# A dense first product from quarters by seven products, the conversion's words in PSUM, and a slot's result copied by ScalarE

## The chip, the cores and the metric

The kernel runs on one core of a Trainium2 chip, as one launch. The metric is the device time of that launch in microseconds. TensorE (PE) multiplies, VectorE (DVE) and ScalarE (ACT) work elementwise on the two on-chip memories SBUF and PSUM, GpSimd (POOL) works on SBUF and issues DMAs, SyncE (SP) issues DMAs. PE's results land in PSUM, which has eight banks.

## What is computed

Three stages follow each other: attention reads of 8 x 8 heads, a routed mixture of 8 experts over 4608 rows, and a dense two-layer network over the same rows:

```python
x = np.ascontiguousarray(attn_out.transpose(0, 2, 1, 3)).reshape(B * S, H * D)   # 4608 x 512
...
for e in range(E):                       # 8 experts, w1 512 x 1024, w2 1024 x 512
    mask = expert_idx == e
    h = np.maximum(x[mask] @ w1[e], 0.0)
    out[mask] = gate_w[mask, None] * (h @ w2[e])
...
h = x @ w_in                             # 4608 x 512 by 512 x 2048
r = np.maximum(h, 0.0)
g = s * (r * r) + b
return (g @ w_out).astype(np.float32)    # 2048 x 512
```

## The kernel before

Products are made of 32-bit values split in two parts, `hi` (what PE's fp32r format holds) and `lo` (the rest): each product is three matmuls, hi-hi, hi-lo and lo-hi, each with a weight load of its own, all accumulated in PSUM. The order on every engine is that in which the code is written.

**Attention and routing** (`phase_a`, to about 140 us) writes the rows sorted by expert to `Xs` in device memory.

**Experts** (`phase_b`, about 140 to 630 us). The rows lie in 38 slots of 128. One turn of the loop over slots (L998) issues: the first product of slot s (`mm1`, 24 matmuls of 512 columns), the columns of slot s+1 (`xcols`: DVE transposes 32 x 32 blocks, L919, ACT copies `hi`, L924, DVE makes `lo`, L925), the second product of slot s-1 (`mm2`, 24 matmuls into `yp`, two buffers), DVE's copy of that result out of PSUM (L975), and the transposes of slot s's hidden values with their parts (`hcols`: PE L949, ACT L954, DVE L955). Beside it POOL loads the experts' weights into a ring of two experts in SBUF, `R[m, part, unit]`, and makes their `lo` parts by `TENSOR_TENSOR` (L702), four operations in a row.

The dense weights come as 64-bit floats and are converted to 32 bits in the same loop, one piece of 512 columns in each of slots 2 to 33 (16 pieces of `w_in`, then 16 of `w_out`): a DMA loads the words into `dbl`, `conv_bits` (L715) makes from the high and low words a value `c_a` and a remainder `c_m` with five DVE operations on SBUF tiles, `conv_split` (L735) makes `hi` (ACT) and `lo` (DVE), and SP's DMAs write both to `Wc` in device memory. When an expert's half of the ring is free, `dense_load` (L749) brings `Wc` into it: `w_in` at the end of the expert stage, `w_out` at the start of the dense one. `dense_done` counts up a semaphore for each quarter, on which PE waits (`wait_prep`).

**Dense** (`phase_c`, from about 630 us). Block 0 has two tiles of 128 rows (256 columns), blocks 1 to 8 four (512 columns). For each of 16 `f` (128 hidden columns) `mm1` (L1104) makes the first product in one of two PSUM buffers: 4 pieces of the inner dimension x 3 matmuls. ACT and DVE make relu, square and the parts `gh`, `gl`; `mm2` (L1125) adds 12 matmuls to `po`, four PSUM buffers, 3 `f` later (`skew`, 5 in block 0). During a block the next block's rows are gathered (POOL), gated (DVE), moved in 32 x 32 blocks (16 DMAs) and transposed (DVE); `ycols` makes their parts. Block 1's columns are transposed by PE instead.

Of the kernel before, what the change touches and what calls it, by code (L numbers as in the profile page):

```python
# [51 lines left out]
class Kern:  # L52
# [4 lines left out]
    def consts(self):  # L57
# [5 lines left out]
        self.Wc = dp.tile([2, 2, P, 8192], F32, name="Wc")  # L63
# [28 lines left out]
        self.flag2 = T([P, 1], "flag2")  # L92
        self.endI = T([1, NE + 1], "endI", I32)
# [621 lines left out]
    def conv_bits(self, c, wp):  # L715

        nc = self.nc
        raw = self.cv[c]
        T = lambda name: wp.tile([P, 512], I32, name="c_" + name, bufs=1)
# [5 lines left out]
        v.tensor_scalar(out=q.bitcast(F32), in0=H.bitcast(F32), scalar1=2.0 ** -112, scalar2=None, op0=ALU.mult)  # L725
        v.tensor_scalar(out=s, in0=H, scalar1=-0x80000000, scalar2=None, op0=ALU.bitwise_and)

        v.scalar_tensor_tensor(out=a, in0=q, scalar=3, in1=s, op0=ALU.logical_shift_left, op1=ALU.bitwise_or)

        v.tensor_scalar(out=s, in0=a, scalar1=-0x800000, scalar2=None, op0=ALU.bitwise_and)  # L730
        b, A = q.bitcast(F32), a.bitcast(F32)
        v.scalar_tensor_tensor(out=b, in0=L, scalar=2.0 ** -36, in1=s.bitcast(F32), op0=ALU.mult, op1=ALU.mult)
        self.cv[c] = A, b

    def conv_split(self, c, wp):  # L735

        nc = self.nc
        v = nc.vector
        m, o = c // 16, (c % 16) * 512
        A, b = self.cv.pop(c)  # L740
        hi = wp.tile([P, 512], F32R, name="c_hi", bufs=1)
        lo = wp.tile([P, 512], F32R, name="c_lo", bufs=1)
        nc.scalar.copy(hi, A)
        v.tensor_tensor(out=A, in0=A, in1=hi.bitcast(F32), op=ALU.subtract)
        v.tensor_tensor(out=lo, in0=A, in1=b, op=ALU.add)
        nc.sync.dma_start(self.Wc[m, 0, :, o:o + 512], hi.bitcast(F32))
        nc.sync.dma_start(self.Wc[m, 1, :, o:o + 512], lo.bitcast(F32))

    def dense_load(self, m, h, wait=False):  # L749

        nc, tc = self.nc, self.tc
        u = h // 2
        if wait:
            c = self.endI[0:1, NE - 2:NE - 1] if m == 0 else self.endI[0:1, NE:NE + 1]
            v = nc.gpsimd.value_load(c, min_val=1, max_val=NSLOT)  # L755
            self.pool_wait(self.d2 if u else self.d1, v)
        x = slice((h % 2) * 2048, (h % 2) * 2048 + 2048)
        for hl in range(2):
            k = nc.gpsimd.dma_start(self.R[:, m, hl, u, x], self.Wc[m, hl, :, h * 2048:(h + 1) * 2048])
# [73 lines left out]
    def places(self, wp):  # L833
# [3 lines left out]
        T = lambda name: wp.tile(B, F32, name="p_" + name)  # L837
# [3 lines left out]
        y, t = V("y"), T("t")  # L841
# [4 lines left out]
        def rows():  # L846
            d = V("d")
# [9 lines left out]
            for nm, w in (("a", wa), ("b", wb), ("c", wc)):  # L857
                v = V(nm)
                nc.vector.tensor_tensor(out=t, in0=self.oh, in1=bc(w), op=ALU.mult)
# [8 lines left out]
        def gates():  # L868
            u, r = V("u"), V("r")
# [15 lines left out]
    def phase_b(self):  # L885
# [6 lines left out]
        with ExitStack() as cx:  # L892
            yps = cx.enter_context(tc.tile_pool(name="yps", bufs=2, space=PSUM))
# [18 lines left out]
            def xcols(s, plain=False):  # L912
# [4 lines left out]
                else:  # L917
                    p = w.tile([P, DM], F32, name="xT", bufs=1)
# [26 lines left out]
            def hcols(s):  # L945
# [4 lines left out]
                hi = w.tile([P, 8, P], F32R, name="hhi")  # L950
                lo = w.tile([P, 8, P], F32R, name="hlo")
# [7 lines left out]
            def mm2(s, ks=range(8)):  # L959
# [15 lines left out]
                nc.vector.tensor_copy(y, p)  # L975
# [16 lines left out]
            places = self.places(wb1)  # L992
# [5 lines left out]
            for s in range(1, NFULL + 1):  # L998
# [24 lines left out]
                if s == C0 + NC:  # L1023
                    z = w.tile([P, DM], I32, name="c_m", bufs=1).bitcast(F32)
# [3 lines left out]
                    for h in range(4):  # L1028
                        self.dense_load(0, h, h % 2 == 0)
                    self.dense_done(0, range(4))  # L1030
# [16 lines left out]
    def phase_c(self):  # L1047
        nc, tc, i = self.nc, self.tc, self.i
        R = self.R
        with ExitStack() as cx:  # L1050
            ops = cx.enter_context(tc.tile_pool(name="ops", bufs=1, space=PSUM))
            h2p = cx.enter_context(tc.tile_pool(name="h2p", bufs=2, space=PSUM))
            t2p = cx.enter_context(tc.tile_pool(name="t2p", bufs=2, space=PSUM))
            w = cx.enter_context(tc.tile_pool(name="wC", bufs=2))
            NF = F2 // P
            blocks = [list(ST)] + [[xt(b, j) for j in range(4)] for b in range(NB)]
            G = {}
# [31 lines left out]
            def ycols(bl, k, first=False):  # L1089
                n = len(bl)  # L1090
                if first:
                    p = t2p.tile([P, 4, P], F32, name="yt")[:, :n, :]
                    for j in range(n):
                        nc.tensor.transpose(p[:, j, :], G["g"][:, j, k * P:(k + 1) * P], self.ident)  # L1094
                else:
                    p = G["yT"][:, :n, :].rearrange("p n (i k t) -> p k n i t", i=4, k=4)[:, k]
                hi = w.tile([P, 4, P], F32R, name="yhi", bufs=4)
                lo = w.tile([P, 4, P], F32R, name="ylo", bufs=4)
                v = lambda a: a[:, :n, :] if first else a[:, :n, :].rearrange("p n (i t) -> p n i t", i=4)
# [4 lines left out]
            def mm1(yt, f, n):  # L1104
                p = h2p.tile([P, 4, P], F32, name="h2")
                for k in range(4):
                    o = (f // 8) * 4096 + k * 1024 + (f % 8) * P
                    win = R[:, 0, :, :, :].rearrange("p a b c -> p (a b c)")
                    hi, lo = win[:, o:o + P], win[:, 8192 + o:8192 + o + P]
                    yh, yl = yt[k][0][:, :n, :], yt[k][1][:, :n, :]  # L1110
                    self.mm(p[:, :n, :], hi, yh, k == 0, False)
                    self.mm(p[:, :n, :], hi, yl, False, False)
                    self.mm(p[:, :n, :], lo, yh, False, k == 3)
                r = w.tile([P, 4, P], F32, name="r2", bufs=3)
                r_ = r[:, :n, :]
                nc.scalar.activation(r_, p[:, :n, :], AF.Relu)  # L1116
                nc.vector.scalar_tensor_tensor(out=r_, in0=r_, scalar=self.s_sb, in1=r_, op0=ALU.mult, op1=ALU.mult)  # L1117
                gh = w.tile([P, 4, P], F32R, name="gh", bufs=6)
                gl = w.tile([P, 4, P], F32R, name="gl", bufs=6)
                nc.scalar.activation(gh[:, :n, :], r_, AF.Identity, bias=self.b_sb, scale=1.0)  # L1120
                nc.vector.scalar_tensor_tensor(out=gl[:, :n, :], in0=r_, scalar=self.b_sb,  # L1121
                                               in1=gh[:, :n, :].bitcast(F32), op0=ALU.add, op1=ALU.subtract)
                return gh, gl

            def mm2(po, g, f, js):  # L1125
                wo = R[:, 1, :, :, :].rearrange("p a b c -> p (a b c)")
                o = f * 512
                hi, lo = wo[:, o:o + 512], wo[:, 8192 + o:8192 + o + 512]
                for j in js:
                    self.mm(po[j], g[0][:, j, :], hi, f == 0, False)  # L1130
                    self.mm(po[j], g[0][:, j, :], lo, False, False)
                    self.mm(po[j], g[1][:, j, :], hi, False, f == NF - 1)
# [12 lines left out]
            for t in range(len(blocks[0])):  # L1145
                gather(blocks[0], t)
            for h in range(4):
                self.dense_load(1, h, h % 2 == 0)
            self.dense_done(1, range(4))
            gated(blocks[0], True)  # L1150
            self.warm(t2p, "yt", 25)
            yt = [ycols(blocks[0], k, True) for k in range(4)]
            for bi, bl in enumerate(blocks):
                n = len(bl)
                nxt = blocks[bi + 1] if bi + 1 < len(blocks) else []
                skew = 5 if bi == 0 else 3
                po = [ops.tile([P, DM], F32, name=f"po{j}") for j in range(n)]
                q = []
                for f in range(NF):
                    if bi == 0 and f % 8 == 0:  # L1160
                        self.wait_prep(2 * (f // 8) + 1)
                    q.append(mm1(yt, f, n))
                    if f >= skew:
                        ff = f - skew
                        if bi == 0 and ff % 4 == 0:
                            self.wait_prep(4 + ff // 4)
                        mm2(po, q[ff], ff, range(n))
                    if 4 <= f < 4 + len(nxt):
                        gather(nxt, f - 4)
                    if f == (9 if bi else 13):  # L1170
# [77 lines left out]
```

## Time and profile before

| | |
|---|---|
| median of 3 runs | 1411.25 us (1409.95 to 1422.62) |
| profiled execution | 1412.1 us, span 1410.3 us from first to last instruction |
| PE busy | 1364.0 us, 97% of the span |
| DVE / ACT / POOL busy | 715.3 / 419.2 / 333.3 us |
| mean granted PE clock | 0.990 |
| moved by DMA | 197.18 MB, mean 140 GB/s |

The matmuls are pipelined: the duration of one in a row is longer than the distance from one to the next, so prices per matmul are taken from the start of the first to the start of the last of many. A DVE operation's row gives its duration; two that do not wait for each other overlap by some hundredths of a microsecond.

### The profile page before, as it was taken

How to read it: one execution, taken by the hardware profiler on the slowest of the kernel's cores; microseconds unless marked ns; L12 is line 12 of the kernel's file. 1: busy time of each engine (PE TensorE's matmuls, PEld its weight loads, DVE VectorE, ACT ScalarE, POOL GpSimd, SP SyncE). 2: the span in 40 equal slices, each digit the busy share in tenths (PEclk: the TensorE clock that was granted, in tenths of full speed). 3: DMA queues.
4: the chain of work that ended last, by engine and by line, in shares of the span. 5: the costliest groups of instructions: out<-in, count | busy, mean ns of one | idle time of the engine just before them, and what ended most of it. 6: DMA issues, size and time to landing. Idle time of an engine off the chain costs nothing.

```text
span 1410.3 us, 19618 instructions
## 1 busy us (share of the span) xinstructions
PE 1364.0 (97%) x6469; PEld 1084.9 (77%) x6469; DVE 715.3 (51%) x1194; ACT 419.2 (30%) x748; POOL 333.3 (24%) x380
## 2 busy tenths in 40 slices
PE   8898999988999989999999999999999999999998
PEld 5666777777778768868888888888888888888887
DVE  6687566888775787423433334233342343433322
ACT  4666222222222222213322223222232232322321
POOL 3777633656430653103001000010000100100000
PEclk9999999999999999999999999999999999999999
DMA  9895886988873895727102021020110201101000
GB/s 331 294 353 188 261 278 222 326 298 296 294 241 123 292 310 172 276 76 287 35 3 58 30 45 46 0 61 30 30 60 0 60 31 28 62 1 31 31 0 30
DMA packets 94289, 197.18 MB, mean 140 GB/s; under 512 B 14952, under 2 KB 49768, under 8 KB 84464
## 3 DMA queue, kind: packets, MB, share of 16 engines
q1 hardware_dynamic: 77776, 98.34, 22.0%
q0 software_dynamic: 16384, 97.53, 19.8%
q8 instruction: 61, 1.00, 0.3%
q14 instruction: 36, 0.29, 0.1%
q10 hardware_dynamic: 32, 0.02, 0.0%
HBM read 140.53 MB, written 47.97 MB: 134 GB/s over the span
## 4 chain that ended last, share of the span: by engine, by line
PE 54%; DMA 0%; issue 0%; DVE 0%; ACT 0%; POOL 0%; POOLq 0%; ACTq 0%
PE h L784 27%; PE po L784 27%; DMA y<-Ys,pos 0%; PE yt L1094 0%; ACT yhi L1100 0%; DVE ob L1136 0%; POOL y L1062 0%; DVE yz L1071 0%; DVE ylo L1101 0%; POOLq L755 0%; POOLq L1062 0%; ACTq L1100 0%
## 5 line engine op out<-in xcount | busy, mean ns | idle before, releaser
L784 PE MATMUL h<-yhi,ring 128*128 128x512 f32 (+1 forms) x1152 | 365.1, 384 | 0.5 <-ACT yhi L1100 0.5
L784 PE MATMUL po<-ring,gh 128*128 128x512 f32 x1088 | 342.7, 396 | 0.0
L1117 DVE SCALAR_TENSOR_TENSOR r<-r,s_sb 128x512 f32<-128x512 f32 (+1 forms) x144 | 103.9, 721 | 330.5 <-ACT r L1116 330.5
L784 PEld LDWEIGHTS h<-yhi,ring 128*128 128x128 f32 x1152 | 214.0, 189 | 47.7 <-ACT yhi L1100 0.7
L784 PEld LDWEIGHTS po<-ring,gh 128*128 128x128 f32 x1088 | 203.7, 188 | 48.2 <-issue 0.2
L784 PE MATMUL h<-ylo,ring 128*128 128x512 f32 (+1 forms) x576 | 221.1, 384 | 0.0
L784 PE MATMUL po<-ring,gl 128*128 128x512 f32 x544 | 215.3, 396 | 0.0
L784 PE MATMUL hp<-ring,xhi 128*128 x592 | 193.3, 408 | 16.2 <-ACT xhi L924 15.3
L1116 ACT ACTIVATE r<-h 128x512 f32<-128x512 f32 (+1 forms) x144 | 83.0, 576 | 377.6 <-PE h L784 377.5
L784 PE MATMUL yp<-ring,hhi 128*128 x592 | 186.7, 396 | 0.0
L702 POOL TENSOR_TENSOR ring<-raw,ring 128x512 fp32r<-128x512 f32 x112 | 149.0, 1362 | 90.8 <-DMA ring<-in_moe_w_dram 90.5
L1062 POOL DMA_INDIRECT y<-Ys,pos x34 | 35.1, 1033 | 542.0 <-DMA yz<-y 333.7
L1121 DVE SCALAR_TENSOR_TENSOR gl<-r,b_sb,gh 128x512 fp32r<-128x512 f32 (+1 forms) x144 | 103.9, 722 | 110.7 <-ACT gh L1120 110.7
L784 PEld LDWEIGHTS hp<-ring,xhi 128*128 128x128 f32 x592 | 111.0, 192 | 42.3 <-ACT xhi L924 17.0
L1120 ACT ACTIVATE gh<-r,b_sb 128x512 fp32r<-128x512 f32 (+1 forms) x144 | 100.9, 701 | 114.0 <-DVE r L1117 114.0
L784 PEld LDWEIGHTS yp<-ring,hhi 128*128 128x128 f32 x592 | 111.5, 189 | 26.9
L784 PEld LDWEIGHTS h<-ylo,ring 128*128 128x128 f32 x576 | 109.0, 189 | 24.3
L784 PEld LDWEIGHTS po<-ring,gl 128*128 128x128 f32 x544 | 102.4, 188 | 25.0
L784 PE MATMUL yp<-ring,hlo 128*128 x296 | 117.9, 398 | 3.7 <-DVE hlo L955 3.7
L784 PE MATMUL hp<-ring,xlo 128*128 x296 | 119.5, 404 | 0.0
L954 ACT CAST hhi<-ht 128x512 fp32r<-128x512 f32 x74 | 43.5, 587 | 161.7 <-PE ht L949 89.1
L955 DVE TENSOR_TENSOR hlo<-ht,hhi 128x512 fp32r<-128x512 f32 x74 | 51.0, 690 | 44.3 <-ACT hhi L954 44.3
(226 smaller groups left out, 1289.9 us busy)
## 6 DMA issues: line engine op xcount, KB each, us to landing
ring<-in_moe_w_dram POOLq DMA_DIRECT2D x32, 1024.0 KB, 9.4
raw<-in_moe_w_dram POOLq DMA_DIRECT2D x28, 1024.0 KB, 5.6
ring<-Wc POOLq DMA_DIRECT2D x16, 1024.0 KB, 12.3
Ys<-y SPq DMA_DIRECT2D x38, 256.0 KB, 2.1
xs<-Xs SPq DMA_DIRECT2D x148, 64.0 KB, 4.4
xT<-in_x_dram SPq DMA_DIRECT2D x16, 512.0 KB, 6.1
xr<-in_x_dram SPq DMA_DIRECT2D x16, 512.0 KB, 7.6
dbl<-in_moe_w_in_dram SPq DMA_DIRECT2D x16, 512.0 KB, 5.5
```

The source lines that it names most:

```text
L702: self.own(nc.gpsimd.tensor_tensor(out=lo[:, x], in0=raw[:, c:c + 512], in1=hi[:, x].bitcast(F32), op=ALU.subtract))
L784: k = nc.tensor.matmul(out, lhsT=l, rhs=r, start=start, stop=stop)
L954: nc.scalar.copy(hi[:, x, :], p[:, x, :])
L955: nc.vector.tensor_tensor(out=lo[:, x, :], in0=p[:, x, :], in1=hi[:, x, :].bitcast(F32), op=ALU.subtract)
L1062: nc.gpsimd.indirect_dma_start(out=G["y"][:, j, :], out_offset=None, in_=self.Ys, in_offset=bass.IndirectOffsetOnAxis(ap=self.pos[:, bl[j] ...
L1116: nc.scalar.activation(r_, p[:, :n, :], AF.Relu)
L1117: nc.vector.scalar_tensor_tensor(out=r_, in0=r_, scalar=self.s_sb, in1=r_, op0=ALU.mult, op1=ALU.mult)
L1120: nc.scalar.activation(gh[:, :n, :], r_, AF.Identity, bias=self.b_sb, scale=1.0)
L1121: nc.vector.scalar_tensor_tensor(out=gl[:, :n, :], in0=r_, scalar=self.b_sb, in1=gh[:, :n, :].bitcast(F32), op0=ALU.add, op1=ALU.subtract)
```

## The change

Lines beginning with "-" are those of before. The diff is cut to what matters for the time.

```diff
 conv_bits:
-        q, a, s = T("m"), T("a"), T("s")
+        a = wp.tile([P, 512], I32, name="c_a", bufs=1)
+        q = self.cps.tile([P, 512], I32, name="cx")
 ...
+        v.tensor_scalar(out=b, in0=H.bitcast(F32), scalar1=2.0 ** -112, scalar2=None, op0=ALU.mult)
+        v.tensor_scalar(out=q, in0=q, scalar1=3, scalar2=None, op0=ALU.logical_shift_left)
+        v.scalar_tensor_tensor(out=a, in0=H, scalar=-0x80000000, in1=q, op0=ALU.bitwise_and, op1=ALU.bitwise_or)
+        v.tensor_scalar(out=q, in0=a, scalar1=-0x800000, scalar2=None, op0=ALU.bitwise_and)
+        v.scalar_tensor_tensor(out=b, in0=L, scalar=2.0 ** -36, in1=b, op0=ALU.mult, op1=ALU.mult)
 conv_split:
+        if 2 <= c < 18:
+            self.conv_parts(self.V[:, 2 * h:2 * h + 2, :], self.Wi[:, i - 1, 4 + 2 * h:6 + 2 * h, :], wp)
+        x = self.cps.tile([P, 2, 256], F32, name="cy")
+        v.tensor_tensor(out=x.rearrange("p a b -> p (a b)"), in0=A, in1=b, op=ALU.add)
 ...
+        self.conv_parts(x, self.Wi[:, i, 2 * h:2 * h + 2, :], wp)
+        if h == 0:
+            nc.scalar.copy(W, x)
+            v.tensor_tensor(out=V[:, 0, :], in0=x[:, 1, :], in1=W[:, 0, :], op=ALU.subtract)
+        else:
+            v.tensor_tensor(out=V[:, 3, :], in0=x[:, 1, :], in1=W[:, 0, :], op=ALU.add)
+            v.tensor_tensor(out=V[:, 1, :], in0=V[:, 3, :], in1=W[:, 1, :], op=ALU.subtract)
+            v.tensor_tensor(out=V[:, 2, :], in0=x[:, 0, :], in1=V[:, 1, :], op=ALU.subtract)
+    def conv_parts(self, x, dst, wp):
+        t = wp.tile([P, 2, 512], F32R, name="c_hl")
 ...
+        nc.scalar.copy(hi, x)
+        nc.vector.tensor_tensor(out=lo, in0=x, in1=hi.bitcast(F32), op=ALU.subtract)
+        nc.sync.dma_start(dst, t.bitcast(F32))
 phase_b:
-            yps = cx.enter_context(tc.tile_pool(name="yps", bufs=2, space=PSUM))
+            yps = cx.enter_context(tc.tile_pool(name="yps", bufs=1, space=PSUM))
+            cps = self.cps = cx.enter_context(tc.tile_pool(name="cps", bufs=1, space=PSUM))
 ...
-                    p = w.tile([P, DM], F32, name="xT", bufs=1)
+                    p = xps.tile([P, 4, P], F32, name="tp").rearrange("p a b -> p (a b)")
 ...
-                nc.vector.tensor_copy(y, p)
+                nc.scalar.copy(y, p)
+                nc.vector.tensor_copy(self.flag3, y[:, DM - 1:])
 phase_c:
+            def sums():
 ...
+                for o, a, b in ((t1, b12, b11), (t2, b22, t1), (t3, b22, b12), (t4, b21, t2)):
+                    nc.gpsimd.tensor_tensor(out=o, in0=a, in1=b, op=ALU.subtract)
+                return b11, t2, t3, t1, b21, t4, b22
+            def mm1(yt, n):
 ...
+                a, b, c, d = [hq.tile([P, 2, HT], F32, name=x) for x in "abcd"]
 ...
+                prod(a[:, 0], A11, B11)
+                nc.scalar.copy(s1[:, 0], a[:, 0])
+                prod(b[:, 0], S2, T2)
+                add(u2[:, 0], s1[:, 0], b[:, 0])
+                prod(c[:, 0], S3, T3)
+                prod(c[:, 1], S1, T1)
+                add(u34, u2.to_broadcast([P, 2, HT]), c)
+                add(y[:, 1], u34[:, 0], c[:, 1])
+                prod(d[:, 0], A22, T4)
+                prod(d[:, 1], S4, B22)
+                add(x, u34, d)
+                prod(a[:, 1], A12, B21)
+                add(y[:, 0], s1[:, 0], a[:, 1])
+            def wload(n):
 ...
+                    nc.sync.dma_start(Rw[:, o:o + WB].bitcast(F32),
+                                      self.Wi[:, n % NP, 1:8, :].rearrange("p q x -> p (q x)"))
 ...
+                skew = 1 if bi else 3
 ...
+                for i in range(NP):
 ...
+                        m = (bi - 1) * NP + i
+                        q.append(mm1(yt, m))
+                        wload(m + NBUF)
+                    if i >= skew:
+                        second(i - skew, range(n))
 ...
+                        if i == 6:
+                            S = sums()
+                if nxt:
+                    yt = ycols(S)
+                for i in range(NP - skew, NP - (not nxt)):
+                    second(i, range(n))
```

In words: the rows of `w_in` and the columns of a block are cut in halves, and for each pair of hidden pieces (`i`, eight pairs) the 2 x 2 product of quarters is formed by seven products of 256 columns and sums before and behind it, instead of eight. A product is `prod`: two pieces of the inner dimension x 3 matmuls. The sums of the weights' quarters are made once, in the conversion (`V`, kept in `Wi` beside the quarters); those of the rows by four POOL subtractions per block (`sums`); those of the results by DVE out of the four banks `a` to `d`. Block 0 keeps the direct first product (`mm1first`). As the seven quarters of all pairs do not fit into the ring, they are streamed from device memory for every block (`wload`, three buffers). Skew is now counted in pairs. The `hhi`/`hlo` tiles of the expert stage have one buffer instead of two.

On DVE, in a slot of the expert stage that converts a piece of `w_in`, there stand before, from one slot's `hlo` to the next (`dbl` are the 64-bit words, the `c_` tiles lie in SBUF):

```order
L725 TENSOR_SCALAR c_m<-dbl 128x512
L726 TENSOR_SCALAR c_s<-dbl 128x512
L728 SCALAR_TENSOR_TENSOR c_a<-c_m,c_s 128x512
L730 TENSOR_SCALAR c_s<-c_a 128x512
L732 SCALAR_TENSOR_TENSOR c_m<-dbl,c_s 128x512
L919 STREAM_TRANSPOSE xT<-xs 128x512
L925 TENSOR_TENSOR xlo<-xT,xhi 128x512
L744 TENSOR_TENSOR c_a<-c_a,c_hi 128x512
L745 TENSOR_TENSOR c_lo<-c_a,c_m 128x512
L975 COPY y<-yp 128x512
L976 ISA
L955 TENSOR_TENSOR hlo<-ht,hhi 128x512 x2
```

and of the change (`cx`, `cy` and `tp` lie in PSUM, `c_v` holds the sums of quarters, `c_w` a copy of two quarters):

```order
L728 TENSOR_SCALAR cx<-dbl 128x512
L729 TENSOR_SCALAR cx<-cx 128x512
L731 SCALAR_TENSOR_TENSOR c_a<-dbl,cx 128x512
L733 TENSOR_SCALAR cx<-c_a 128x512
L734 SCALAR_TENSOR_TENSOR cx<-dbl,cx 128x512
L956 STREAM_TRANSPOSE tp<-xs 128x512
L962 TENSOR_TENSOR xlo<-tp,xhi 128x512
L771 TENSOR_TENSOR c_hl<-c_v,c_hl 128x2x256
L750 TENSOR_TENSOR cy<-c_a,cx 128x512
L771 TENSOR_TENSOR c_hl<-cy,c_hl 128x2x256
L759 TENSOR_TENSOR c_v<-cy,c_w 128x256
L1015 COPY flag_92<-y 128x1
```

The copy of the slot's result has left DVE, three operations on the quarters' sums have come (in every other slot five), and the words' intermediate results have moved to PSUM.

On PE, at the start of a full dense block, the change has at the end of `mm1(0)` and the beginning of `mm1(1)` (`a` to `d` are the banks of the products, `ring` the weights, or the columns' parts that lie behind them):

```order
L820 MATMUL d<-ring 128x256 [waits Activation_49]
L820 MATMUL d<-ring 128x256 [waits DVE_49]
L820 MATMUL d<-ring 128x256 x4
L820 MATMUL a<-ring 128x256 [waits Activation_49]
L820 MATMUL a<-ring 128x256 x5
L820 MATMUL a<-yh_11034,ring 128x256 [waits DMAHW0_49,DVE_49]
L820 MATMUL a<-yl_11035,ring 128x256
```

where before, one `f` after another alternated between two buffers:

```order
L784 MATMUL h_11519<-yhi,ring 128x512 [waits Activation_49]
L784 MATMUL h_11519<-ylo,ring 128x512
L784 MATMUL h_11519<-yhi,ring 128x512 x2
L784 MATMUL h_11519<-ylo,ring 128x512
L784 MATMUL h_11519<-yhi,ring 128x512 x2
```

The bank `a` that the last product of one pair fills is the first that the next pair fills again, with no other matmul between them here.

On POOL, the dense stage before has only gathers (`L1062 DMA y<-Ys,pos`, 32 in a row). The change has for each block:

```order
L1166 TENSOR_TENSOR yz<-y 128x512
L1166 TENSOR_TENSOR yz<-y,yz 128x512
L1166 TENSOR_TENSOR yz<-y 128x512
L1166 TENSOR_TENSOR yz<-y,yz 128x512
L1105 DMA y<-Ys,pos 128x512 x4
```

Four subtractions on SBUF tiles have come between the gathers of one block and those of the next.

## Rows read from the trace of the kernel before

**Rows 1.** Stretches: length, busy time (instructions) of each engine, clock, DMA share, GB/s.

```profile
160.00:395.00 235.00, 222.40 (x1003) 178.14 (x1002) 186.70 (x211) 59.59 (x107) 125.75 (x132) 0.99 0.83 282
395.00:560.00 165.00, 158.56 (x718) 127.36 (x717) 121.57 (x159) 42.63 (x77) 57.43 (x59) 0.99 0.67 227
...
315.00:340.00 25.00, 21.10 (x89) 16.79 (x88) 19.54 (x21) 6.12 (x11) 18.20 (x18) 0.93 0.94 337
515.00:540.00 25.00, 21.22 (x92) 16.76 (x91) 22.08 (x22) 5.62 (x10) 17.93 (x17) 0.93 0.76 269
...
640.00:682.00 42.00, 42.00 (x273) 38.69 (x274) 18.00 (x39) 15.35 (x34) 9.83 (x15) 0.97 0.59 213
682.00:772.00 90.00, 90.00 (x390) 72.43 (x389) 30.64 (x45) 23.91 (x37) 4.17 (x4) 1.00 0.13 30
```

**Rows 2.** The chain that ended last, in order of time: start, length, what.

```profile
778.51 11.21 PE h L784 x48
...
795.32 2.81 PE po L784 x12
...
868.23 11.21 PE h L784 x48
```

**Rows 3.** Timeline of one expert slot: start, us, engine, line, operation [idle before <-releaser].

```profile
278.39 5.79 DVE L728 SCALAR_TENSOR_TENSOR c_a<-c_m,c_s 128x512 int32<-128x512 int32 x1
278.62 5.00 POOL L702 TENSOR_TENSOR ring<-raw,ring 128x512 fp32r<-128x512 f32 x4
...
281.83 1.04 PE L949 MATMUL ht<-ident,h 128*128 128x128 f32 x8
...
285.37 0.70 DVE L919 STREAM_TRANSPOSE xT<-xs 128x512 f32<-128x512 f32 x1
...
286.75 0.69 DVE L925 TENSOR_TENSOR xlo<-xT,xhi 128x512 fp32r<-128x512 f32 x1 [0.68 <-ACT xhi L924]
286.77 0.73 PE L784 MATMUL hp<-ring,xhi 128*128 x2 [3.90 <-ACT xhi L924]
```

**Rows 4.** Three DVE lines in 160 to 560 us: duration ns min/median/max, first and last start.

```profile
L728 DVE SCALAR_TENSOR_TENSOR c_a<-c_m,c_s x31: 691/693/5805, 160.9 to 552.1; 128x512 int32<-128x512 int32 x31
...
L730 DVE TENSOR_SCALAR c_s<-c_a x31: 426/428/1549, 162.6 to 552.8; 128x512 int32<-128x512 int32 x31
...
L955 DVE TENSOR_TENSOR hlo<-ht,hhi x60: 679/691/694, 171.6 to 550.7; 128x512 fp32r<-128x512 f32 x60
```

**Rows 5.** PE's timeline in block 0: first and last of 19 such rows.

```profile
643.13 0.28 PE L784 MATMUL h<-ylo,ring 128*128 128x256 f32 x1
...
649.61 0.28 PE L784 MATMUL h<-ylo,ring 128*128 128x256 f32 x1
```

**Rows 6.** DVE and ACT, 640 to 1411 us: shapes xcount | busy us, mean ns | idle before.

```profile
L1117 DVE SCALAR_TENSOR_TENSOR r<-r,s_sb 128x512 f32<-128x512 f32 x128 | 96.1, 751 | 316.2 <-ACT r L1116 316.2
...
L1101 DVE TENSOR_TENSOR ylo<-yt,yhi 128x256 fp32r<-128x256 f32 x1 | 0.4, 414 | 0.0
...
L1120 ACT ACTIVATE gh<-r,b_sb 128x512 fp32r<-128x512 f32 x128 | 92.8, 725 | 104.8 <-DVE r L1117 104.8
```

**Rows 7.** DVE's timeline at the end of two undisturbed slots.

```profile
596.30 0.69 DVE L975 COPY y<-yp 128x512 f32<-128x512 f32 x1 [1.63 <-PE yp L784]
597.80 0.69 DVE L955 TENSOR_TENSOR hlo<-ht,hhi 128x512 fp32r<-128x512 f32 x1 [0.80 <-ACT hhi L954]
599.14 0.69 DVE L955 TENSOR_TENSOR hlo<-ht,hhi 128x512 fp32r<-128x512 f32 x1 [0.66 <-ACT hhi L954]
...
608.42 0.69 DVE L975 COPY y<-yp 128x512 f32<-128x512 f32 x1 [2.04 <-PE yp L784]
```

**Rows 8.** POOL's subtractions of L702 alone, in a stretch: length, busy time (instructions).

```profile
160.00:395.00 235.00, 100.34 (x77) 0.99 0.83 282
```

**Rows 9.** DMA issues: how many, KB each, median us from issue to landing.

```profile
dbl<-in_moe_w_in_dram SPq DMA_DIRECT2D x16, 512.0 KB, 5.5
```

More of the change, by code (lines that the diff above doesn't have):

```diff
@@ L846, in rows @@
         def rows():
-            d = V("d")
+            d, t = V("d"), T()
             nc.vector.tensor_copy(d, self.desti)
@@ L1102, in ycols, with ycols0 @@
                 return hi, lo
-            def mm1(yt, f, n):
-                p = h2p.tile([P, 4, P], F32, name="h2")
+            def ycols0(n):
+                yt = []
                 for k in range(4):
[L1107 to L1123, printed above, removed]
@@ new lines, in ycols0 @@
+                    for j in range(n):
+                        nc.tensor.transpose(p[:, j, :], G["g"][:, j, k * P:(k + 1) * P], self.ident)
+                    if k % 2 == 0:
+                        t = [w.tile([P, 2, HT], F32R, name=f"y{x}{k // 2}", bufs=1) for x in "hl"]
+                    hi, lo = [a[:, k % 2, :n * P].rearrange("p (a b) -> p a b", b=P) for a in t]
+                    nc.scalar.copy(hi, p)
+                    nc.vector.tensor_tensor(out=lo, in0=p, in1=hi.bitcast(F32), op=ALU.subtract)
@@ new lines, in wload, with mm2 @@
+            def wload(n):
+                if n < NP * NB:
+                    o = (n % NBUF) * WB
+                    nc.sync.dma_start(Rw[:, o:o + WB].bitcast(F32),
+                                      self.Wi[:, n % NP, 1:8, :].rearrange("p q x -> p (q x)"))
+            def mm2(po, g, i, js):
+                for u in range(2):
+                    o = (2 * i + u) * 512
+                    hi, lo = Ro[:, o:o + 512], Ro[:, 8192 + o:8192 + o + 512]
+                    first, last = i == 0 and u == 0, i == NP - 1 and u == 1
+                    for j in js:
+                        gh, gl = [a[:, j % 2, :] for a in g[u][j // 2]]
+                        self.mm(po[j], gh, hi, first, False)
+                        self.mm(po[j], gh, lo, False, False)
+                        self.mm(po[j], gl, hi, False, last)
@@ L1176, in phase_c, with second @@
-                yt = []
-                for ff in range(NF - skew, NF):
-                    if nxt and len(yt) < 4:
-                        yt += [ycols(nxt, len(yt), bi == 0), ycols(nxt, len(yt) + 1, bi == 0)]
-                    if bi == 0 and ff % 4 == 0:
-                        self.wait_prep(4 + ff // 4)
-                    if nxt:
-                        mm2(po, q[ff], ff, range(n))
+                def second(i, js):
+                    if bi == 0 and i % 2 == 0:
+                        self.wait_prep(4 + i // 2)
+                    mm2(po, q[i], i, js)
```

236 lines of the change are left out of this document (146 added, 90 removed).

## The prediction

> **What bounds the kernel now.** I read the stretches first, then the chain that ended last, then the timeline inside one slot and one dense block. TensorE (PE) is the bound nearly everywhere. From 682 us on it is never idle at the full clock [rows 1], and the chain is nothing but its matmuls: 48 matmuls of a first product (`h`) take 11.21 us, 12 of a second (`po`) 2.81 us, and a whole block repeats every 868.23 - 778.51 = 89.72 us [rows 2]. So a 512-column matmul with its own weight load costs 2.81/12 = 0.234 us, and a pair of `f` (24 `h`, 24 `po`) 11.22 us. Here only fewer PE microseconds help, or new waits hurt.
>
> The expert stage is PE-bound with holes. From 160 to 395 us PE is busy 222.40 of 235 us, from 395 to 560 us 158.56 of 165 [rows 1]: 12.6 and 6.4 us idle. The clock falls with the longest holes: 0.93 in two stretches of 25 us [rows 1], each 0.07 x 25 = 1.75 us of full-speed work lost. Together 14.4 us before 395 us and 8.2 behind.
>
> What makes a hole is seen at 278 us [rows 3]: the conversion's DVE operation L728, all of whose operands lie in SBUF, lasts 5.79 us because POOL runs four subtractions (5.00 us) meanwhile; the columns of the next slot come late, and PE stands 3.90 us. L728 takes 691 ns at best and 5805 at worst; L955, with one operand in PSUM, 679 to 694 [rows 4].
>
> **The first product by seven products.** A pair now issues 7 x 2 x 3 = 42 matmuls of 256 columns in place of 24 of 512; its 24 matmuls of the second product stay. The price of 256 columns is in the trace, because block 0 holds two token tiles: from 643.13 to 649.61 us lie 18 groups of three, 0.36 us each [rows 5], 0.120 us a matmul, with a weight load each and the same order hi-hi, hi-lo, lo-hi. A pair's first product falls from 5.61 to 42 x 0.120 = 5.04 us; 64 pairs: **-36.5 us**. Columns alone would promise one eighth of 5.61, 0.70; the smaller matmul gives 0.13 of it back.
>
> The 16 PE transposes that made block 1's columns go, since block 1 now comes by DVE as the others do; at 1.04/8 = 0.13 us [rows 3]: **-2.1 us**.
>
> A new wait: the four product banks have one buffer each, and the first matmul of each `mm1` after a block's first waits for DVE's add of bank `a`, the last of the `mm1` before. Mostly 24 `po` matmuls (5.61 us) lie between. At a block's start they do not, since the skew is one pair and `mm1(0)` is followed by `mm1(1)`. From the start of the last matmul: 0.28 us to its end (a 256-column row [rows 5]), 0.1 to the add, 0.41 for it (the 256-column difference [rows 6]), 0.05 back, less the 0.12 that PE would have needed: 0.75 us, in 8 blocks **+6 us**. Behind that add on DVE stand the squares; the copies of the finished block stand ahead of it, but have 4 us of products to hide in.
>
> Behind a block's last `mm1(7)` only one `po` group of 5.61 us lies before `po` needs its squares. From the last matmul's start: adds to 0.8, relu of x and y (about 0.6 each, as ACT's copy inside the 0.68 of [rows 3]) to 1.0 and 1.6, then alternately square 0.75, ACT 0.725, difference 0.75 [rows 6], for x first, then y: y's difference ends at 5.6. It is asked for at 0.12 + 5.61 + 0.47 = 6.2. So 0.55 us to spare, and nothing is lost unless POOL interferes: its four new subtractions start when DVE's last transpose of the next block ends, about 7.0 us after the end of `mm1(6)`, 3.6 before the end of `mm1(7)`. At 5.00 us for four [rows 3] they end at +1.4, and DVE's square of x, with both inputs in SBUF, wants to start at +1.0. Bounds: nothing, or the whole burst in front (5.00 - 0.55 = 4.5 us). I take the near end, 0.3, in 7 blocks **+2 us**.
>
> Adds, splits and gate fit: DVE per pair 3 x 0.41 + 2 x 0.69 + 4 x 0.75 = 5.6 us, and some 1.4 as a share of the block's work, of 10.65. Weights now stream: 128 x 3584 x 4 B = 1.835 MB per pair, with two `mm1` and three `po` groups (26.9 us) from issue to need; the dense stage has the DMA share free (0.13 [rows 1]). I cost it at nothing. Block 0's six gathers on POOL instead of two put the loads of the second weights some 4 us later; three pairs of skew cover that.
>
> Dense stage: -36.5 - 2.1 + 6 + 2 = -30.6 us.
>
> **The conversion.** One slot takes 608.42 - 596.30 = 12.12 us of PE [rows 7]. The new DVE queue of a slot that converts first weights, uncontended: five word operations, each waiting for the one before. No row has PSUM on both sides; the SBUF one-input form takes 428 ns [rows 4], the copy out of PSUM 0.69 [rows 7]; I take the latter for all, 5 x 0.73 with the hop = 3.65. Transpose to difference 1.38, ACT's copy included [rows 3]; three operations that follow without a wait at some 0.62 = 1.86; the word's sum and ACT's copy of it 0.69 + 0.68; the quarters' sums 1.2 (one and three of 0.41, with hops and the copy of W); the flag 0.15; the two `hlo` 599.14 + 0.69 - 597.80 = 2.03 [rows 7]. Sum 11.6 us of 12.12, against some 8.6 before the change. The change thus buys freedom from POOL with DVE time.
>
> Here the Trainium skill speaks against the edit: "VectorE: DVE Perf Modes", section "Why PSUM operands drop a tier", says that an fp32 one-input operation loses its double rate as soon as an operand is in PSUM. The trace agrees for reads (428 against 690 ns); by the rule three word operations lose 0.26 us each, which the 0.73 above holds already, and by the row at the old rate the slot would be 10.9.
>
> Contention that is left: the differences of the sums (`c_v` and `c_hl` both in SBUF) in every such slot, and one sum in every other. POOL's subtractions fill 100.34 of 235 us [rows 8] in bursts of 5 us: an operation that meets them at random waits 0.43 x 2.5 = 1.07 us. That is 1.6 a slot: 13.2 against 12.12, over 16 slots 18 us, of which some 4 are covered (the columns are ready 4 us early in an undisturbed slot). So 14 us of holes before 395 us, as now (14.4): **no gain there**. Behind 395 us, where the second weights convert, nothing has both inputs in SBUF and the queue is short (under 10 us): the 8.2 us go, **-8.2 us**. The bounds are 0 and -22.6.
>
> The slot's result by ACT (0.6 for DVE's 0.69) lies beside `mm1` of the next slot; with one `yp` buffer it is bare only before the last slot, where two second products follow each other: +0.7; the first half's 14 against 14.4 gives 0.4 of it back: **+0.3 us**.
>
> **Sum.** 1412.1 (the profiled execution, 0.9 over the median) - 30.6 - 8.2 + 0.3 = 1373.6; I say 1374.
>
> **Rivals.**
> *The expert stage clears fully.* If POOL's bursts miss the sums, both halves' 22.6 us go: 1412.1 - 30.6 - 22.6 + 0.7 = 1360. For it: a slot that is late by 4 us costs PE nothing. Against: 11.6 of 12.12 leaves no room to catch up.
>
> *DVE becomes the bound of the first half.* If PSUM operations take 0.8 instead of 0.73, or word loads come late (512 KB land in 5.5 us [rows 9] while the stage's DMA share is already 0.83 [rows 1], and 8 MB more are written), a slot grows by another 0.8 us: 16 x 0.8 = 13 us worse: 1387. For it: the queue is 96% full by my own sum.
>
> *POOL's burst stands in the dense chain.* If it lasts twice as long on strided operands, or starts later, each of 7 blocks loses 4.5 us and the clock some 1.75 us as in the holes above [rows 1]: 1374 + 7 x 6 = 1416: no gain left.
>
> *The weights' stream becomes the bound* (slower than before). If a transfer of 1.835 MB takes longer than a pair, three buffers do not help. From 11.3 us on (10.65, and the 39 us of gains over 61 pairs) the kernel is slower than before. At the rate of the word loads (512 KB in 5.5 us [rows 9]) it would be 19 us, and the time 1374 + 61 x 8.6 = 1900. Against: at 640 to 682 us the queues moved 213 GB/s with a share of 0.59 [rows 1], so about 360 when full, 5.1 us.
>
> *The small matmul is bound by its weight load.* From 5.61/42 = 0.134 us a matmul on, seven products gain nothing; at 0.150 they lose 64 x 0.69 = 44 us, in all 1455. Rows 5 have 0.120 with such loads, so the chance is small. The Trainium skill, "TensorE: Matmul & The Clock Gate", section "Back-to-back issue gap", gives for streams of loads and matmuls 81 ns at 128 columns and 131 at 512; an estimate between them, 98 at 256, would make a pair's first product 0.96 us longer. The trace differs: 234 at 512 columns, 120 at 256.
>
> **How the numbers follow.** As summed 50%; expert stage clear 12%; DVE the bound 28%; burst in the chain 6%; stream 3%; small matmul 1%. The three first are faster by over 1% (under 1397, about what a measurement of this kernel can tell from no change): 0.90; same 0.06; slower 0.04. The likeliest case alone reaches from 1364 to 1384 (0 to 1.5 us at each block's end, first half 4 us either way). Two in ten left out: 1357 to 1393.
>
> **What would show it.** Pitch of a dense block 85.2 us and a little more; 42 first-product matmuls in 5.04 us; a PE wait for DVE's add of about 0.75 us once a block; little or no wait of `po` behind a block's end. In the expert stage no DVE operation over 1 us except those on `c_v`, PE whole behind 395 us, and PE waits for `xhi` or `hlo` before it. Wrong would be: 256-column matmuls above 0.125 us, PE waiting for the ring's DMA, or waits behind the POOL sums.

## The result, and the profile after

The changed kernel takes **1362.7 us** (median; 1361.6 to 1364.7), the kernel before 1411.9 beside it: ratio **0.9646**, 95% interval 0.9607 to 0.9685. Forecast was 1374, between 1357 and 1393. Measured again it took 1364.3 (1360.2 to 1367.1; 0.9661, 0.9630 to 0.9691). The profiled execution spans 1359.7 us, 50.6 less than before's 1410.3.

The stretches of [rows 1], now of the kernel after (length, busy time and instructions of PE, PEld, DVE, ACT, POOL, clock, DMA share, GB/s):

```profile
160.00:395.00 235.00, 229.98 (x1063) 188.26 (x1062) 171.54 (x273) 86.57 (x157) 117.22 (x128) 0.99 0.90 322
395.00:560.00 165.00, 165.00 (x771) 135.47 (x770) 99.51 (x159) 54.15 (x95) 56.95 (x64) 1.00 0.71 244
640.00:682.00 42.00, 38.12 (x233) 32.60 (x232) 21.35 (x30) 11.41 (x20) 12.50 (x12) 1.00 0.69 236
682.00:772.00 90.00, 89.49 (x549) 79.98 (x548) 57.31 (x96) 30.29 (x52) 9.74 (x8) 1.00 0.59 220
```

From 395 to 560 us PE has no hole left, as forecast. Before that it stands 5.0 us, not the 12.6 of [rows 1] that I forecast to stay. The third row, which held only block 0 before, now holds its end and the change to block 1, with 3.9 us of holes. Timeline, PE's first matmul of the dense stage, before and then after:

```profile
639.81 0.55 PE L784 MATMUL h<-yhi,ring 128*128 128x256 f32 x1 [0.45 <-ACT yhi L1100]
```
```profile
618.74 0.55 PE L820 MATMUL a<-yh,ring 128*128 128x256 f32 x1 [0.36 <-issue]
```

So the dense stage went from 1410.3 - 639.81 = 770.5 to 1359.7 - 618.74 = 741.0: **-29.5 us, forecast -30.6**. All before it gained 639.81 - 618.74 = **21.1 us, forecast 7.9**. There lies the miss, 13.2 us, of which the dense stage takes 1.1 back; by medians it is 1374 - 1362.7 = 11.3. Not all of the 21.1 is the expert stage's: PE's first expert matmul starts at 148.40 us before and at 147.34 after, so 1.1 us lie in the attention stage, which the change leaves alone, and 20.0 in the expert stage.

The chain of a dense block, to compare with [rows 2] (start, length, what):

```profile
761.81 0.97 PE a L820 x6
...
772.66 0.71 PE a L820 x6
773.37 0.71 PE b L820 x6
774.08 1.43 PE c L820 x12
775.51 1.44 PE d L820 x12
776.95 0.72 PE a L820 x6
777.67 5.58 PE po L820 x24
783.25 0.71 PE a L820 x6
...
847.29 0.97 PE a L820 x6
```

A pair's 42 products run from 772.66 to 777.67, 5.01 us or 0.119 each (summed: 5.04), a pair 10.59 us, a block 847.29 - 761.81 = 85.48 us (before 89.72; forecast 85.2 and a little more, which by the sum's own waits is 86.2). The 24 `po` matmuls take 5.58 us where before they took 5.61.

PE's waits, in total, times, longest; first the expert stage of before, then after's, then after's dense stage:

```profile
PE hp L784 <- ACT xhi L924: 15.3, 7, 3.9
PE yp L784 <- DVE hlo L955: 3.7, 3, 1.2
```
```profile
PE yp L820 <- POOLq L637: 5.0, 1, 5.0
PE ht L986 <- ACT h L979: 1.8, 1, 1.8
PE hp L820 <- ACT hhi L993: 0.8, 1, 0.8
PE hp L820 <- ACT xhi L961: 0.8, 1, 0.8
PE yp L820 <- ACT y L1014: 0.7, 1, 0.7
...
PE a L820 <- DVE r L1214: 6.1, 8, 1.6
PE po L820 <- ACT gh L1177: 1.4, 1, 1.4
```

Between 160 and 560 us the columns' waits (`xhi`, `hlo`) have gone in both halves, also before 395 us, where the forecast named them as a sign. The one wait that is left there, 5.0 us, is for expert weights; the four short ones lie outside that stretch. In the dense stage the wait for bank `a` is there eight times, 6.1 us in all (summed: 6).

### The profile page after: what moved, and what is told of

Same layout as the page of the kernel before. It is cut to its first block, busy times and chain, and to the rows that moved or that the text cites. A ratio compares the mean times of both kernels' runs of the same rounds, so it can differ in the third digit from the quotient of the medians.

```text
span 1359.7 us, 22750 instructions
## 1 busy us (share of the span) xinstructions
PE 1316.9 (97%) x7605; PEld 1114.1 (82%) x7605; DVE 841.2 (62%) x1574; ACT 481.4 (35%) x882; POOL 367.7 (27%) x404
## 4 chain that ended last, share of the span: by engine, by line
PE 50%; DMA 2%; DVE 1%; POOL 1%; issue 0%; SPq 0%; ACT 0%; DVEq 0%; POOLq 0%; ACTq 0%
PE po L820 26%; PE a L820 7%; PE d L820 7%; PE c L820 7%; PE b L820 4%; DMA yz<-y 1%; POOL yz L1166 0%; DMA out_dram<-ob 0%; DVE r L1214 0%; SPq L1125 0%; DMA y<-Ys,pos 0%; DVE ob L1256 0%; DVE u L1214 0%; DVE y L1130 0%; DVE y L1116 0%
## 5 line engine op out<-in xcount | busy, mean ns | idle before, releaser
L1178 DVE SCALAR_TENSOR_TENSOR gl<-r,b_sb,gh 128x512 fp32r<-128x512 f32 x136 | 102.3, 753 | 107.8 <-ACT gh L1177 107.8
L1233 ACT ACTIVATE r<-r 128x512 f32<-128x512 f32 x128 | 73.8, 624 | 239.4 <-DVE r L1214 239.4
L1177 ACT ACTIVATE gh<-r,b_sb 128x512 fp32r<-128x512 f32 x136 | 98.5, 725 | 133.7 <-DVE r L1174 133.7
L1174 DVE SCALAR_TENSOR_TENSOR r<-r,s_sb 128x512 f32<-128x512 f32 x136 | 103.3, 759 | 31.6 <-ACT r L1233 20.0
L820 PE MATMUL c<-ring 128*128 128x256 f32 x768 | 102.3, 283 | 0.7 <-DVE ring L1139 0.7
L820 PE MATMUL d<-ring 128*128 128x256 f32 x768 | 102.8, 283 | 0.1
L820 PEld LDWEIGHTS d<-ring 128*128 128x128 f32 x768 | 96.8, 192 | 0.3 <-DVE ring L1139 0.3
L820 PEld LDWEIGHTS c<-ring 128*128 128x128 f32 x768 | 96.0, 190 | 0.9 <-DVE ring L1139 0.9
L979 ACT ACTIVATE h<-hp 128x512 f32<-128x512 f32 x74 | 40.2, 596 | 106.1 <-PE hp L820 106.0
L820 PE MATMUL a<-yh,ring 128*128 128x256 f32 x320 | 70.3, 289 | 6.4 <-DVE r L1214 6.1
```

The costliest lines, as they stand in the source:

```text
L820: k = nc.tensor.matmul(out, lhsT=l, rhs=r, start=start, stop=stop)
L979: nc.scalar.activation(h[:, n, :], p[:, n, :], AF.Relu)
L1174: nc.vector.scalar_tensor_tensor(out=r, in0=r, scalar=self.s_sb, in1=r, op0=ALU.mult, op1=ALU.mult)
L1177: nc.scalar.activation(gh, r, AF.Identity, bias=self.b_sb, scale=1.0)
L1178: nc.vector.scalar_tensor_tensor(out=gl, in0=r, scalar=self.b_sb, in1=gh.bitcast(F32), op0=ALU.add, op1=ALU.subtract)
L1233: nc.scalar.activation(flat(r), flat(r), AF.Relu)
```

## The experiments

**What do POOL's bursts cost the kernel before?** Its subtractions for the experts are left out, and the low halves come by DMA:

```diff
-                raw = raws.pop(0)
-                for c in range(0, 2048, 512):
-                    ... lo[:, x] = raw - hi on POOL
+                self.own(nc.gpsimd.dma_start(lo[:, h * 2048:(h + 1) * 2048], src))
```

> The kernel before, with POOL's subtractions for the experts' weights left out: the low halves are loaded by DMA from the weights themselves, the same bytes in place of the raw loads, so the experts' results leave the low parts wrong and only the time is read. It measures what POOL's bursts cost the kernel before. If they are the cause of its holes: the 14.4 us before 395 us and the 8.2 behind go, 1412 - 22.6 = 1389 us, no word operation above 0.8 us, as where the words lie in PSUM (1388). If the holes come from a full DVE queue or late columns: 1405 to 1412, with the xhi waits still there.

Measured: 1385.4 us (ratio 0.9810, 0.9771 to 0.9849), 26.5 below the 1411.9 of the kernel before, measured beside it. PE from 160 us on:

```profile
160.00:395.00 235.00, 235.00 (x1086) 191.35 (x1085) 140.13 (x235) 63.19 (x116) 30.80 (x82) 1.00 0.87 296
```

No hole, full clock, and L728 at 691 to 695 ns. Without the bursts the holes of before are gone, so DVE's queue alone does not make them. The run gained 4 us more than the 22.6 of the holes and the clock; where those come from stays open.

**Do the temporaries in PSUM alone do as much?** In the kernel before, only:

```diff
-        q, a, s = T("m"), T("a"), T("s")
+        q = self.cps.tile([P, 512], I32, name="cx")    # PSUM; words in the order of the kernel after
...
-        v.tensor_tensor(out=A, in0=A, in1=hi.bitcast(F32), op=ALU.subtract)
-        v.tensor_tensor(out=lo, in0=A, in1=b, op=ALU.add)
+        x = self.cps.tile([P, 512], F32, name="cy")    # A + b in PSUM, then hi by ACT, lo = x - hi
...
-                    p = w.tile([P, DM], F32, name="xT", bufs=1)
+                    p = xps.tile([P, 4, P], F32, name="tp").rearrange("p a b -> p (a b)")
```

> The kernel before, with its dense stage untouched; only the expert stage's words, their sum and the columns' transpose go to PSUM (one yp buffer makes the banks free), and the slot's result stays a DVE copy. Theory 1 (the expert stage gained about 20 us, and it is the temporaries in PSUM that did it): 1412 - 20 = 1392 us, the xhi and hlo waits of PE between 160 and 580 us gone, no word operation above 1 us. My prediction's own form (nothing gained before 395 us, 8.2 us behind): 1404. Rival (the gain comes from ACT's copy of the slot's result or from the dense part): 1411 to 1413.

Measured: 1388.0 us (0.9827, 0.9785 to 0.9869), 24.8 below before. The first stretch:

```profile
160.00:395.00 235.00, 235.00 (x1086) 191.35 (x1085) 157.05 (x233) 66.23 (x117) 124.70 (x137) 1.00 0.88 302
```

PE is whole here, and from 395 to 580 us too. The bursts still run (POOL busy 124.70 us), and the word operation that is L728 here takes 694 to 697 ns throughout.

**And undone in the kernel after?**

```diff
-        q = self.cps.tile([P, 512], I32, name="cx")
+        q = wp.tile([P, 512], I32, name="c_q", bufs=1)
```

> The kernel after, with only the words (tile cx, five operations a slot) back in SBUF; their sum, the transpose and ACT's copy of the result stay as changed. Theory 1 (words in PSUM end the holes): the words meet POOL's bursts again, L728 and its neighbours last up to 5 us, the xhi waits of PE return in both halves, and the time is 1363 + 14 to 20 = 1377 to 1383 us. Rival (the other edits of the stage did it): 1362 to 1366; a word is faster in SBUF (0.43 for 0.69 us) so it might even be 1360.

Measured: 1403.1 us (0.9928, 0.9900 to 0.9956): 40 us worse than after, twice what was expected. The source view of a word operation (ns min/median/max) and PE's waits in the expert stage:

```profile
L729 DVE TENSOR_SCALAR c_q<-c_q x32: 426/428/5753, 159.4 to 578.2; 128x512 int32<-128x512 int32 x32
...
PE hp L820 <- ACT xhi L961: 24.9, 8, 5.7
PE yp L820 <- ACT hhi L993: 3.3, 2, 2.5
```

A word in SBUF is 0.26 us faster when nothing meets it, and lasts up to 5.75 us when a burst does. With the longer queue of the seven-product conversion the holes are larger than before's (clock 0.96 before 395 us, 0.97 behind). Of the change's expert part this line is the one that carries it; without it the change would have been worth 10 us, not 49.

**How full is DVE's queue?** Two doses. The result of a slot copied by DVE again (+0.54 us a slot):

```diff
-                nc.scalar.copy(y, p)
-                nc.vector.tensor_copy(self.flag3, y[:, DM - 1:])
+                nc.vector.tensor_copy(y, p)
```

> The kernel after, with the slot's result copied out of PSUM by DVE again (0.69 us there in place of a 0.15 us flag, 0.54 us more in DVE's queue of a slot). If the queue is as full as summed (11.7 us of 12.12, with 0.6 us of waits for POOL measured): 0.7 us a slot too long over 16 slots, 4 us covered, so about +7: 1370 us, with new xhi waits before 395 us. If DVE's idle quarter is real slack: 1362 to 1364, no new waits.

and two idle operations in each converting slot (+1.46 us):

```diff
+        for _ in range(2):
+            v.tensor_scalar(out=q, in0=q, scalar1=-1, scalar2=None, op0=ALU.bitwise_and)
```

> The kernel after, with two extra DVE operations in each converting slot (an AND with all ones on the words in PSUM, 0.73 us each, 1.46 us a slot; the values do not change). This doses what I mis-sized: POOL cost 0.6 us a slot where I had taken 1.6. If the queue is full at 12.12 us: (11.7 + 0.6 + 1.46 - 12.12) x 16 - 4 = +22 us before 395 us, nothing behind, 1385 us, with xhi waits in the W_in half only. If DVE has slack (27% idle in 160 to 395 us): at most +3, 1366 us.

Measured: 1365.6 us (1 to 3 above after, within the spread of its executions) and 1379.7 (15 to 17 above). The second, first stretch and PE's waits:

```profile
160.00:395.00 235.00, 220.97 (x987) 174.27 (x986) 187.24 (x292) 78.53 (x144) 115.11 (x126) 0.99 0.86 307
...
PE hp L822 <- ACT xhi L963: 7.9, 11, 1.3
```

The second dose went as its first theory said, with less time lost than the 22 us expected. The first did not: PE has no `xhi` wait before 395 us in its trace, as its rival said. Its dose is also smaller than 0.54 us a slot. Two of its slots that meet no burst take 11.90 us (three sums of quarters) and 11.73 (one); in the second kind the copy only fills time in which DVE waited for ACT's `hhi`.

The queue itself is best read from the second dose's trace, where DVE falls behind and works without a pause other than its waits for ACT. One slot is from transpose to transpose; these two meet no burst, the first with three sums, the second with one. Then PE's slot in the kernel after, by the same operation in a stretch where PE is whole:

```profile
204.00 0.72 DVE L958 STREAM_TRANSPOSE tp<-xs 128x512 f32<-128x512 f32 x1
...
216.82 0.72 DVE L958 STREAM_TRANSPOSE tp<-xs 128x512 f32<-128x512 f32 x1
...
230.04 0.71 DVE L958 STREAM_TRANSPOSE tp<-xs 128x512 f32<-128x512 f32 x1
```
```profile
457.95 0.72 DVE L956 STREAM_TRANSPOSE tp<-xs 128x512 f32<-128x512 f32 x1
...
469.98 0.72 DVE L956 STREAM_TRANSPOSE tp<-xs 128x512 f32<-128x512 f32 x1
```

The slots take 12.82 and 13.22 us; less the dose of 1.46 they are 11.36 and 11.76, **11.56 on the mean**, without contention. My sum had 11.6. PE's slot is 12.03 us, not the 12.12 of [rows 7].

That PE's slot became 0.09 us shorter is a gain that I had not forecast and cannot explain: it is 12.03 in the kernel after also with the words in SBUF, and 12.12 in the kernel before also with the temporaries in PSUM. Over the stage it makes some 3 of the 20.0 us.

**Is it the queue that leaves the rest?** Heavy words (first weights) alternate with light ones (second weights):

```diff
+            seq = [c for k in range(16) for c in (k, 17 + k)[:2 if 0 < k < 14 else 1]] + [16, 17, 31]
-                    self.conv_load(c + 1, w)    # conv_bits(c, w), conv_split(c, w) likewise
+                    self.conv_load(seq[c + 1], w)
```

> The kernel after, with the thirty-two words converted in mixed order: from the third word on a word of the first weights (long DVE queue, 11.7 us and POOL's 0.6) alternates with one of the second (under 10 us, nothing with both inputs in SBUF). Total work and bytes are the same. If the first half's queue is full by my sum, a light slot now takes up what a heavy one leaves over: the remaining waits of PE for columns and expert weights before 395 us (5 to 6 us and the clock's 0.99) go, 5 to 7 us less than after in this call. If those waits come from DMA or from chance alone: within 2 us of after.

> The kernel after, unchanged, for the spread of its own executions and as the measure beside which the mixed order and the earlier moves are read: 1361 to 1366 us, with executions up to 5 us apart where an expert's weights or a slot's columns come late in one and not in the other.

Measured: 1361.1 (1359.7 to 1361.9) against 1364.3 (1360.2 to 1367.1) for the unchanged kernel after, measured beside it. The first stretch is whole:

```profile
160.00:395.00 235.00, 235.00 (x1092) 192.31 (x1091) 168.53 (x264) 83.54 (x150) 125.93 (x137) 1.00 0.91 319
```

3.2 us, less than the 5 to 7 expected, since some of what was saved came back later (1 us behind 395 us). The late expert weights are gone with it. In the kernel after they look like this (POOL, then PE):

```profile
298.88 5.03 POOL L704 TENSOR_TENSOR ring<-raw,ring 128x512 fp32r<-128x512 f32 x4 [10.86 <-DMA ring<-in_moe_w_dram]
...
310.93 1.22 PE L820 MATMUL yp<-ring,hhi 128*128 x2 [5.02 <-POOLq L637]
```

Under the mixed order POOL waited 8.9 us there for the same transfer. Whether the lighter DVE queue or the better spread of the conversion's stores did that, this run does not separate.

**Can the wait for bank `a` be taken away?** In a block's second pair the banks change places:

```diff
-                a, b, c, d = [hq.tile([P, 2, HT], F32, name=x) for x in "abcd"]
+                a, b, c, d = [hq.tile([P, 2, HT], F32, name=x) for x in ("cbad" if i == 1 else "abcd")]
```

> The kernel after; in the second pair of every block the four product banks are taken in the order c, b, a, d, so that its first product starts in a bank that the pair before freed long ago. Theory: the waits of PE for DVE's add there (0.51 us in six blocks, 1.42 and 1.58 in two, together 6.1 us in the profile of after) go: 1363 - 4 to 6 = 1357 to 1359. Rival (the wait only moves to the squares, which hang on the same adds, or to bank d or b): 1362 to 1363.

Measured: 1363.9 us (0.9644, 0.9615 to 0.9672), no gain; the rival held, at another place than it named. PE's waits and ACT's timeline:

```profile
PE c L820 <- ACT s L1219: 4.1, 8, 0.7
...
770.03 0.72 ACT L1177 ACTIVATE gh<-r,b_sb 128x512 fp32r<-128x512 f32 x1 [1.48 <-DVE r L1174]
770.66 0.35 ACT L1219 COPY s<-c 128x256 f32<-128x256 f32 x1
```

The pair's seventh product now waits 0.45 to 0.7 us, since it shares a bank with the first, and ACT's copy of the first stands behind the squares of the pair before. So the wait was moved, not removed: it now ends with a copy that stands in ACT's queue behind that pair's squares.

**Block 0.** Block 1's gating and moves are issued ahead of the first streamed loads:

```diff
+                        if i == 0:
+                            gated(nxt)
+                            blocks32()
                         if i in (1, 3, 5):
                             wload(i // 2)
...
-                        if i == 3:
+                        if i == 3 and bi:
```

> The kernel after; in block 0 the gating and the sixteen block-moving DMAs of block 1 are issued after the first pair, ahead of the first loads of streamed weights, not after the fourth pair behind two loads of 1.8 MB. Theory: block 1's columns come early, and the 3.7 us that PE stands at the change from block 0 to block 1 in the profile of after go, or nearly: 1359 to 1361. Rival (the sums or the gathers, not the DMAs, are late, or the first weights now come late in their place): 1362 to 1365.

Measured: 1356.3 us (0.9601, 0.9570 to 0.9631). Stretch 640 to 682 us:

```profile
640.00:682.00 42.00, 41.49 (x264) 37.41 (x263) 26.97 (x39) 13.88 (x24) 11.16 (x9) 1.00 0.72 265
```

PE gained 41.49 - 38.12 = 3.4 us there, as the first theory said; the rest of the 6 to 8 lies within the spread of executions (1351 to 1364). That the loads ahead in SP's queue made the moves late is not what the traces show. The sixteen moves on SP's queue and what SP waited for ahead of them, in the kernel after, then the moves in this run:

```profile
636.54 20.59 SPq L1125 DMA_DIRECT2D yz<-y  x16
...
SPq L1125 <- DVE y L1116: 4.7, 1, 4.7
```
```profile
623.27 20.05 SPq L1125 DMA_DIRECT2D yz<-y  x16
```

In the kernel after, SP had issued both loads by 631.54 us and then waited 4.7 us for DVE's gating. Issuing the moves took about as long with the loads ahead (20.59 us) as without (20.05). So what came late was the gating, issued after the fourth pair; this run moved it forward together with the moves.

Bank order and block 0 together, and mixed order and block 0 together:

> The bank order and the earlier moves of block 1 together. If the two waits are independent: 1363 - 6 - 3 = 1354 us, between 1353 and 1357. If one lateness hides behind the other (the 1.42 us of block 1 belong to both): 1356 to 1358.

> The mixed order of words and the earlier moves of block 1 together. If both act by themselves: 3.5 us at block 1 and 5 to 7 us in the first half, 1353 us in the mean and less spread than block 1's moves alone showed (1351 to 1364). If the mixed order gives nothing: 1356 to 1360, with the same spread.

Measured: 1358.0 (1351.6 to 1363.1), no better than block 0 alone; and **1356.3** (1354.5 to 1358.2; ratio 0.9611, 0.9583 to 0.9639) against 1364.3 for the kernel after, measured beside it. Every execution of it is faster than every one of that. It is as fast as block 0 alone, with about a quarter of the spread (3.6 us for 13.3).

**The stream.** Each load of streamed weights is issued twice:

> The kernel after, with every load of streamed weights issued twice, into the same place (3.67 MB a pair in place of 1.835). It doses the transfer that I costed at nothing. By the dense stage's own rows (215 GB/s at a DMA share of 0.52 to 0.58, so about 390 when full) the doubled stream wants 388 GB/s and stands just at the limit: 1363 to 1395 us, with the first PE waits for the ring's DMA. If one queue gave no more than the word loads seemed to (512 KB in 5.5 us): far over 1900.

Measured: 1532.6 us, 170 above after. What SP waited for from 700 to 1400 us, and that stretch:

```profile
SPq L1241 <- DMA ring<-Wi: 481.3, 52, 13.9
...
700.00:1400.00 700.00, 584.32 (x3497) 523.91 (x3496) 352.25 (x586) 185.62 (x320) 55.71 (x48) 0.91 0.79 302
```

The second load writes where the first does, and SP issues it only when the first has landed: 52 such waits, 481.3 us. So the run shows what two loads one after the other cost (3.67 MB in 13.3 us a pair on the mean), and not how much room a single stream has. Nor does it speak against the 5.1 us that I took from the DMA share: 302 GB/s at a share of 0.79 make about 380 when full, 213 at 0.59 made 360. What is shown of the single stream is that PE never waited for it.

## Why the prediction was right or wrong

The sign, the range and the dense stage were right, with these terms: the 256-column price (0.119 for 0.120), the wait for bank `a`, the stream (never waited for). That the bank's wait came to 6.1 for 6 is in part luck: its own terms add up to 0.72 us and not 0.75, and it was 0.51 us in six blocks and 1.4 and 1.6 in two. So is the stage's -29.5 for -30.6. At the pitch shown, eight blocks gave 8 x (89.72 - 85.48) = 33.9 us where the sum had 28.5, since POOL's burst at block ends cost nothing (I had +2) and a pair took 10.59 for 10.65; the rest of the stage lost 4.4 where the sum had a gain of 2.1. Of that, 3.7 us are the change from block 0 to block 1, which I had not costed: the waits of block 1's columns, 1.36 + 0.21 + 0.71 + 1.42. The first of them, and POOL's wait for DVE's transposes:

```profile
661.30 0.74 PE L820 MATMUL po<-ring,gh 128*128 128x512 f32 x2 [1.36 <-ACT gh L1177]
...
663.39 1.64 POOL L1166 TENSOR_TENSOR yz<-y 128x512 f32<-128x512 f32 x1 [9.69 <-DVE y L1130]
```

The moves of block 1's columns began late, since its gating was issued only after the fourth pair of block 0; with gating and moves issued after the first pair, these waits shrink to 0.5 us.

**The step that failed** is "14 us of holes before 395 us, as now: no gain there". Its mechanism (a queue close to PE's slot, plus what still meets POOL) is borne out by the second dose, and its queue of 11.6 us by the slots read there (11.56). The term that was too large is the contention. DVE's rows from 160 to 560 us (busy, mean ns):

```profile
L771 DVE TENSOR_TENSOR c_hl<-c_v,c_hl 128x512 fp32r<-128x512 f32 x16 | 17.4, 1090 | 0.0
...
L762 DVE TENSOR_TENSOR c_v<-c_v,c_w 128x256 f32<-128x256 f32 x8 | 6.2, 773 | 0.3
```

Undisturbed they take 0.682 and 0.425 us, so contention is (1.090 - 0.682) x 16 + (0.773 - 0.425) x 8 = 9.3 us, **0.58 a slot for the 1.6 summed** (0.69 in the second profile of the same kernel). Eight of the 24 operations met a burst, 0.33 for the 0.43 assumed; a meeting cost 1.2 us on the mean, not the 2.5 of half a burst. So a slot of DVE takes 11.56 + 0.58 = 12.14 us, where the sum had 13.2, against PE's 12.03: over 16 slots 2 us, less than the 4 that I had as covered, and no hole from the columns is left. The 5.0 us that PE still stands are the wait for expert weights, a term that I did not have.

The same working gives the second dose: its rows have 0.71 us of contention a slot, so 11.56 + 1.46 + 0.71 = 13.73 us; 14 slots of its trace (178.24 to 370.33 us) take 13.72 each. Over 16 slots that is 27 us beyond PE's, 23 less the 4 covered, and 18 less the 5.0 for expert weights, a wait that its trace does not have: 15 to 17 were measured. The 4 us remain an estimate.

Near such an edge a miss of 1 us a slot decides over 14 us, and to state one side of it was wrong. The outcome lies beside the rival "clears fully" (1360), to which I gave 12%. Its condition held in part: a third of the operations did meet a burst, but for too short a time to matter. The likeliest case alone reached down to 1364 only; that 1362.7 lies within the stated range is owed to the range's covering this rival too.

What the rule of the Trainium skill ("VectorE: DVE Perf Modes", section "Why PSUM operands drop a tier") charges was paid: one-input words take 0.69 us with an operand in PSUM and 0.43 in SBUF. The trace agrees, and the words' run shows that here it was worth paying.

## What to carry to other kernels

Where another engine's bursts hold up DVE, an operand in PSUM that makes each operation 0.26 us slower can still be the fastest form, as it was here, where none of these operations waited. When a queue's sum comes out within a tenth of its period, price the outcomes on both sides of the edge, and measure the margin with a dose before believing either; then read the queue slot by slot in the dose's trace, since the time alone mixes it with what was covered. A dose has to be checked in its trace too: one of those here vanished in half of the slots, another made its queue wait for itself. When a transfer comes late, look first at what its queue waited for.

## What was not expected of the hardware

A DVE operation held up by POOL does not always wait for the end of the burst, by which I mean POOL's four subtractions in a row. Timelines of two meetings:

```profile
186.05 5.04 POOL L704 TENSOR_TENSOR ring<-raw,ring 128x512 fp32r<-128x512 f32 x4
188.23 3.41 DVE L771 TENSOR_TENSOR c_hl<-c_v,c_hl 128x512 fp32r<-128x512 f32 x1
...
274.09 5.24 POOL L704 TENSOR_TENSOR ring<-raw,ring 128x512 fp32r<-128x512 f32 x4 [9.66 <-DMA ring<-in_moe_w_dram]
276.57 1.59 DVE L762 TENSOR_TENSOR c_v<-c_v,c_w 128x256 f32<-128x256 f32 x1
```

The first ends at 191.64, after the whole burst (191.09). The second ends at 278.16, with more than a microsecond of the burst to go, and that burst is 0.2 us longer than the first: by these rows it got in between two of POOL's operations, though the row does not show their single ends. What decides this was not tried.
